# A hand-written planner orders the last stage of a three-stage kernel with a second set of machine constants and rules

## The chip, the cores and the metric

The kernel runs on one core of one Trainium2 chip. The metric is the device time of one execution in microseconds, here the median of three runs. Traces are of one profiled execution. The engines are called as the profile calls them: PE does matmuls (PEld is its weight loads), DVE, ACT and POOL do element-wise work, SP issues DMAs. Each engine runs its own list of instructions strictly in the order in which the program holds them, and semaphores make an instruction wait for work of other engines.

## What is computed

Three stages follow one another. The third is the one that the change is about.

```python
def _attn_ref(q, k, v):            # 4 x 8 heads, 576 positions, 64 wide, window of 128
    scores = where(mask, scale * q @ k.T + bias, -1e9)
    return softmax(scores) @ v
def _moe_ref(x, w_in, w_out):      # 2304 tokens, 512 -> 2048 -> 512
    h = np.maximum(x @ w_in, 0.0)
    return h * h @ w_out
def _moe2_ref(x, w_gate, w1, w2):  # 8 experts, 512 -> 1024 -> 512, all tokens through all
    P = sinkhorn(exp(x @ w_gate))  # 8 rounds
    out = 0
    for e in range(8):
        h = np.maximum(x @ w1[e], 0.0)
        out += P[:, e:e + 1] * (h @ w2[e])
    return out
```

## The kernel before

Nearly every fp32 matrix is held as two fp16 ones, a high and a low half, and a product is three fp16 matmuls (high-high, high-low, low-high). In the third stage each matrix product is done with seven block products in place of eight (sums and differences of blocks are formed first), so that PE does less and DVE, ACT and POOL do more.

**The third stage.** There are 16 groups `g` (8 experts in two halves), each with two parts `p`, and five blocks of tokens `j` (4, 2, 4, 4, 4 tiles of 128). For each `g, j, p`, `plan_pair` makes one pass: seven block products on PE (`g_prod`, L1450, six matmuls each) into the PSUM banks X, Y and Z; copies out of a bank by ACT (`g_copy`, L1478); additions of a bank to such a copy by DVE (`g_add`, L1482), on which the next product waits; relu and the high half by ACT (L1492, L1501, L1522); the low half by DVE (`g_lo`, L1526, from SBUF; `g_lo_bank`, L1505, straight from a bank); four running sums by POOL (`g_sum`, L407 and L1512). Seven output products follow for each block (`o_prod`, L1545, one after the other by a chain of dependences); DVE adds them into the result (`o_add`, L1571). Beside this the weights of the next group are prepared (`weights`): loaded (L1309), squared and summed for a scale (L1317), split in a high half by ACT (`ex_hi`, L1346) and a low half by DVE (`ex_lo`, L1350), with four block sums by POOL between the first and the second split (`ex_sums`, L1360 and L407). `gates` (L1682, L1683) makes the factors of a group on DVE.

**What sets the order.** Nothing is ordered by hand. Every piece of work is a `Unit` with an engine, a cost in us, a rank, the units it comes after, and the buffers it takes. `Plan.run` plays through a model of the machine: whenever an engine is free, it starts the ready unit of lowest rank. The order in which units start in this play is the order in which they are emitted, and so the order on each engine. Products have ranks that rise with `g`, `j` and `p`; the element-wise work of a pass has the first rank (`GEMM`); the preparation of weights comes last (9000 and up). Units `shared` (all of POOL's and those of DVE named in `PORT`: `g_lo`, `ex_lo` and others) exclude each other in the play: one that another engine's shared unit overlaps waits for its end. The result of a unit reaches its own engine after `own_lag` and another engine after `lags`. Buffers limit how far the play may run ahead: `h=2` banks (X, Y), `av=1` (Z), `y=4` (output banks), `hp=24` half pairs, `t=10` copies.

Costs are written as `c_pe(6, 256)` = 6 x (256/2400 + 0.0022) = 0.653 us for a product, `c_dve(n)` = 0.07 + 1.04 n/1000, `c_act(n)` = 0.18 + 0.83 n/1000 (0.18 replaced where a second number is given), `c_pool(n)` = 0.12 + 1.93 n/1000.

Of the kernel before, what the change touches and what calls it, by code (L numbers as in the profile page):

```python
# [18 lines left out]
class Unit:  # L19
    def __init__(self, engine, cost, emit, rank, lag, until):  # L20
        self.engine, self.cost, self.emit, self.rank, self.lag, self.until = engine, cost, emit, rank, lag, until
        self.name = ""
        self.waits, self.then, self.takes, self.nth, self.frees = 0, [], [], [], []
        self.shared = False


class Plan:
# [6 lines left out]
    def __init__(self, slots, queues):  # L34
        self.slots = slots
        self.queues = {tag: [] for tag in queues}
        self.units = []
        self.lags, self.own_lag = {}, {}
        self.got = {}

    def add(self, engine, cost, emit, after=(), rank=0, take=(), lag=None, until=None):
        u = Unit(engine, cost, emit, rank, self.lags.get(engine, 0.1) if lag is None else lag, until)
# [23 lines left out]
    def run(self):  # L66
        room = dict(self.slots)
        ready, free_at, events = {}, {}, []
        order, seq = [], 0

        def fits(u):
# [11 lines left out]
        held, until = None, 0.0  # L83
        while left:
            moved = True
            while moved:
                moved = False
                for eng, units in ready.items():
                    if free_at[eng] > now:
                        continue  # L90
                    fit = [
                        u for u in units if fits(u) and not (u.shared and held is not eng and until > now + 1e-6)
                    ]
# [4 lines left out]
                    if u.shared:  # L98
                        held, until = eng, now + u.cost
                    if u.until is not None and now > u.until:  # L100
                        u.cost, u.emit = 0.0, lambda: None
                    for t in u.takes:
# [3 lines left out]
                    free_at[eng] = now + u.cost  # L106
                    heapq.heappush(events, (now + u.cost, seq, eng, None))
                    heapq.heappush(events, (now + u.cost + self.own_lag.get(eng, u.lag), seq + 1, eng, (u, True)))
                    heapq.heappush(events, (now + u.cost + u.lag, seq + 2, eng, (u, False)))
                    seq += 3  # L110
# [7 lines left out]
            while events and events[0][0] <= now:  # L118
                u = heapq.heappop(events)[3]
                if u is None:  # L120
                    continue
                u, same = u
                for t in () if same else u.frees:
                    t[1] -= 1
                    room[t[0]] += not t[1]
                for x in u.then:
                    if same != (x.engine is u.engine):
                        continue
# [19 lines left out]
def kernel(  # L148
# [165 lines left out]
    def make_tail():  # L314
# [1033 lines left out]
    def ex_lo(g, kind, p, x):  # L1348
        for t, hi, lo in ex_parts(g, kind, p, x):
# [403 lines left out]
    def plan_pair(g, j, p, z, after, prev):  # L1753
# [3 lines left out]

        def split(name, *after):
# [6 lines left out]
                DVE, c_dve(n, 1.25 if of_bank else 1.04), g_lo_bank if of_bank else g_lo, g, j, p, name,  # L1765
                rank=GEMM, after=[hi],
            )
            fs[name] = (hi, lo)
            return lo

        def relu(x, after, **kw):
            return unit(ACT, c_act(n, 0.07), g_relu, g, j, p, x, rank=GEMM, after=[after], **kw)

        def total(name, *after):
            return unit(POOL, c_pool(n) + 0.08, g_sum, g, j, p, name, rank=GEMM, after=after)
# [3 lines left out]
        def prod(x, y, after, take=()):  # L1779
            return unit(PE, cost, g_prod, g, j, p, x, rank=z + 14 * y, take=take, after=after)  # L1780

        def copy(x, after):
            return unit(ACT, c_act(n, 0.06), g_copy, g, j, p, x, rank=GEMM, take=["t"], after=[after])

        def add(x, *after):
            return unit(DVE, c_dve(n), g_add, g, j, p, x, rank=GEMM, after=after)
# [41 lines left out]
    def plan_experts(closed, opened, lgt, routed):  # L1828
# [6 lines left out]
        def weights(g, kind):  # L1835
# [10 lines left out]
            us = chain(DVE, [0.14] + [TINY] * 3, ex_scale, g, kind, rank=z, after=[al])  # L1846
# [3 lines left out]
            for p in range(NP):  # L1850
# [8 lines left out]
                us.append(unit(DVE, c_dve(W, 1.17), ex_lo, g, kind, p, 1, rank=z + p, after=[hi]))  # L1859
# [82 lines left out]
    with tc.manual_schedule():  # L1942
# [33 lines left out]
        opened = unit(SP, 0.0, open_banks, after=[closed, *(u for us in ready_y.values() for u in us)])  # L1976
# [31 lines left out]
```

## Time and profile before

| | us |
|---|---|
| median of 3 runs (1927.27 to 1929.2) | 1928.04 |
| the profiled execution | 1927.08 |
| its span, first to last instruction | 1924.8 |
| PE busy in the span | 1887.3 |
| DVE busy in the span | 1540.3 |
| ACT, POOL busy in the span | 1239.8, 937.1 |

The profiled execution lies 0.96 us under the median and 2.28 us over its own span. Busy time of PE is the time in which at least one matmul is shown under way; a matmul's bar is longer than the distance to the next one, so that a run of matmuls is read by its starts. An idle time is put down to the work that released the instruction behind it.

### The profile page before, as it was taken

The numbers are of one execution on the slowest core, as the hardware profiler recorded it, in microseconds if no ns is written. First come the engines' busy times: TensorE is split into PE (matmuls) and PEld (weight loads), VectorE is DVE, ScalarE is ACT, GpSimd is POOL, SyncE is SP. The second block draws the span as 40 slices with busy tenths as digits, with TensorE's granted clock in tenths as the row PEclk, the third lists the DMA queues.
The fourth block names the chain that finished last, engine by engine and source line by source line (L and its number), as shares of the span: only waits on it lengthen the run. The fifth ranks groups of instructions, "written<-read, shape, count | busy, mean of one in ns | idle before, by whom it ended". The sixth has DMA issues, their size and how long they took to land.

```text
span 1924.8 us, 47113 instructions
## 1 busy us (share of the span) xinstructions
PE 1887.3 (98%) x18458; PEld 1681.8 (87%) x18458; DVE 1540.3 (80%) x3876; ACT 1239.8 (64%) x3434; POOL 937.1 (49%) x1198
## 2 busy tenths in 40 slices
PE   9999999999998999999999999999999999999998
PEld 9888888888887888898988889898888889888897
DVE  6796575454349889898988989899898889989877
ACT  5777577354356877676766667676666667666653
POOL 3444354347436655454545545454554545455432
PEclk9999999999999999999999999999999999999999
DMA  9454274220010100010100101010010101000002
GB/s 242 123 138 113 57 128 78 39 57 1 1 45 12 45 23 23 23 45 12 34 19 28 34 15 43 13 34 23 23 34 20 38 13 34 23 24 12 2 23 77
DMA packets 159662, 85.35 MB, mean 44 GB/s; under 512 B 112080, under 2 KB 144848, under 8 KB 159440
## 3 DMA queue, kind: packets, MB, share of 16 engines
q1 hardware_dynamic: 159440, 82.35, 17.0%
q8 instruction: 144, 2.36, 0.5%
q14 instruction: 78, 0.64, 0.1%
HBM read 64.50 MB, written 4.72 MB: 36 GB/s over the span
## 4 chain that ended last, share of the span: by engine, by line
PE 84%; DVE 10%; ACT 2%; DMA 2%; issue 1%; SPq 0%; POOL 0%; DVEq 0%; ACTq 0%; POOLq 0%
PE oX L1545 17%; PE X L1450 17%; PE oY L1545 9%; PE h L1036 9%; PE y L1075 8%; PE Y L1450 8%; PE Z L1450 5%; PE oZ L1545 4%; DVE hp L1526 3%; PE s L593 1%; PE warm L291 1%; DVE late L1350 1%; PE av L654 1%; DVE acc_wd L1571 1%; PE t L569 1%
## 5 line engine op out<-in xcount | busy, mean ns | idle before, releaser
L1450 PEld LDWEIGHTS <-late 128*128 128x128 f16 x6720 | 617.2, 98 | 89.5 <-issue 24.8
L1545 PEld LDWEIGHTS <-hp 128*128 128x128 f16 x6048 | 584.9, 98 | 64.9
L1545 PE MATMUL oX<-late,hp 128*128 128x256 f16 x3456 | 465.4, 273 | 0.0
L1450 PE MATMUL Y<-y,late 128*128 128x256 f16 (+1 forms) x1920 | 241.3, 262 | 5.1 <-DVE hp L1505 3.8
L1526 DVE TENSOR_TENSOR hp<-late,hp 128x256 f16<-128x256 f32 (+1 forms) x501 | 235.9, 485 | 5.6 <-ACT hp L1522 4.2
L1545 PE MATMUL oY<-late,hp 128*128 128x256 f16 x1728 | 235.2, 273 | 0.0
L1075 PE MATMUL y<-sq,w_out 128*128 128x256 f16 x1728 | 216.7, 273 | 1.4 <-DVE yacc L1089 0.9
L1036 PE MATMUL h<-xT,w_in 128*128 128x256 f16 x1728 | 215.9, 274 | 0.0
L1522 ACT ACTIVATE hp<-late 128x256 f16<-128x256 f32 (+1 forms) x501 | 193.8, 393 | 26.1 <-POOL late L407 13.8
L407 POOL TENSOR_TENSOR sq<-r,sq 128x256 f16<-128x256 f32 x144 | 105.1, 732 | 215.8 <-ACT sq L1061 214.5
L1450 PE MATMUL X<-late 128*128 128x256 f16 (+1 forms) x1728 | 204.9, 255 | 1.1 <-DVE late L1482 0.5
L407 POOL TENSOR_TENSOR stage<-stage 128x256 f32<-128x256 f32 x210 | 166.6, 799 | 75.4 <-DVE late L1350 64.2
L1036 PEld LDWEIGHTS <-w_in 128*128 128x128 f16 x1728 | 168.1, 98 | 20.8 <-issue 0.2
L1075 PEld LDWEIGHTS <-w_out 128*128 128x128 f16 x1728 | 166.2, 98 | 22.5 <-issue 2.4
L1450 PE MATMUL X<-form,late 128*128 128x256 f16 x1152 | 157.1, 272 | 13.6 <-DVE x L1482 6.9
L1350 DVE SCALAR_TENSOR_TENSOR late<-stage,es,late 128x512 f16<-128x512 f32 (+2 forms) x180 | 164.1, 937 | 0.6 <-ACT late L1346 0.5
L1492 ACT ACTIVATE late<-late 128x256 f32<-128x256 f32 (+1 forms) x206 | 79.7, 393 | 127.8 <-DVE late L1482 126.4
L1526 DVE TENSOR_TENSOR hp<-x,hp 128x256 f16<-128x256 f32 (+1 forms) x299 | 151.5, 516 | 3.2 <-ACT hp L1522 1.4
L1346 ACT ACTIVATE late<-stage,es 128x512 f16<-128x512 f32 (+2 forms) x180 | 135.6, 787 | 8.5 <-POOL stage L407 8.4
L407 POOL TENSOR_TENSOR late<-late 128x256 f32<-128x256 f32 (+1 forms) x167 | 126.6, 759 | 10.2
L1512 POOL TENSOR_TENSOR late<-late 128x256 f32<-128x256 f32 (+1 forms) x60 | 40.6, 677 | 182.4 <-DVE hp L1526 166.3
L1053 DVE SCALAR_TENSOR_TENSOR r<-h,unit_s,r 128x256 f32<-128x256 f32 x96 | 46.0, 480 | 101.6 <-ACT r L1045 101.1
(237 smaller groups left out, 3445.8 us busy)
## 6 DMA issues: line engine op xcount, KB each, us to landing
stage<-in_moe_w_dram SPq DMA_DIRECT2D x60, 256.0 KB, 3.2
stage<-in_moe_w_dram SPq DMA_DIRECT2D x30, 512.0 KB, 3.6
st_in<-in_moe_w_in_dram SPq DMA_DIRECT2D x16, 512.0 KB, 7.1
st_out<-in_moe_w_out_dram SPq DMA_DIRECT2D x16, 512.0 KB, 5.3
raw_q<-in_q_dram SPq DMA_DIRECT2D x16, 256.0 KB, 4.0
raw_k<-in_k_dram SPq DMA_DIRECT2D x16, 256.0 KB, 4.1
raw_v<-in_v_dram SPq DMA_DIRECT2D x16, 256.0 KB, 4.6
out_dram<-acc_wc SPq DMA_DIRECT2D x8, 256.0 KB, 2.3
```

Source lines behind the costliest of these rows:

```text
L407: POOL.tensor_tensor(out=dst, in0=src, in1=hi, op=ALU.subtract)
L1036: PE.matmul(hp, lhsT=w[:, a, kk, r], rhs=xT[parts1[m][0]][:, b, kk, c : c + MC], start=(kk == 0 and a == b), stop=(kk == KD - 1 and a == LO),)
L1053: DVE.scalar_tensor_tensor(out=r, in0=h if m > 1 else r, scalar=s, in1=r, op0=ALU.mult, op1=ALU.mult)
L1075: PE.matmul(hold["y", m, d // 2][:, d % 2], lhsT=w[:, a, f % FPC, d * P : (d + 1) * P], rhs=sq[:, b], start=(first and d % 2 == 0 and a == ...
L1346: ACT.activation(out=hi, in_=t, func=ACTF.Copy, scale=es[:, g, 2 * kind + 1 : 2 * kind + 2])
L1350: DVE.scalar_tensor_tensor(out=lo, in0=t, scalar=es[:, g, 2 * kind + 1 : 2 * kind + 2], in1=hi, op0=ALU.mult, op1=ALU.subtract)
L1450: PE.matmul(pt, lhsT=w[:, a, row(kk), :], rhs=rhs, start=(x in (1, 2, 5) and kk == 0 and a == c), stop=(x in (2, 3, 4) and kk == KH - 1 an ...
L1492: ACT.activation(out=t, in_=src, func=ACTF.Relu)
L1512: POOL.tensor_tensor(out=c, in0=c, in1=b, op=ALU.add)
L1522: ACT.activation(out=f[:, HI], in_=hold["t", PLACE[name], g, j, p], func=ACTF.Copy)
L1526: DVE.tensor_tensor(out=f[:, LO], in0=hold["t", PLACE[name], g, j, p], in1=f[:, HI], op=ALU.subtract)
L1545: PE.matmul(pt[:, t], lhsT=f[:, a, t * P : (t + 1) * P], rhs=w[:, c, row], start=(x in (1, 2, 5) and p == t == 0 and a == c), stop=(x in ( ...
```

## The change

The planner gets a second set of constants and three more rules; no instruction is added, dropped or altered, and only the order of instructions on the engines can differ.

- A `Model` holds the time that a result takes to another engine (`cross`) and to its own (`own`), a `lead` and a flag `turns`. The first model has the constants of before, lead 0 and no turns. `EXACT` has other constants, a lead of 0.065 us and turns. It takes over in the play when `open_banks` starts, that is when the last block of the second stage is split.
- `bank`: a unit that touches bank X, Y or Z of a pass can't start in the play while another engine's use of that bank, with its lag, is not over. This holds in both models.
- `lead`: a shared unit may start 0.065 us before the end of the one that it waits for. `turns`: an engine that has been refused the port goes before one that asks later.
- Costs: the low half from a bank 0.39 to 0.336 us (256 columns); relu 0.07 to 0.06 (bank) or 0.1 (SBUF) in its fixed part; `ex_lo`'s first split becomes two units of 512 and 256 columns in place of one (costed with 1024 or 768); `ex_scale` 0.14 + 3 x 0.08 to 4 x 0.07; sums on POOL 0.08 to 0.07 in the fixed part; `gates` 0.3 to 0.95.

```diff
+class Model:
+    def __init__(self, cross, own, lead, turns):
+        self.cross, self.own, self.lead, self.turns = cross, own, lead, turns
...
         def fits(u):
-            return all(
+            eng, until = banks.get(u.bank, (u.engine, 0.0))
+            if eng is not u.engine and until > now + 1e-6:
+                return False
+            if not all(
                 room[t[0]] > n and (t[0] not in self.queues or self.queues[t[0]][n] is u)
                 for t, n in zip(u.takes, u.nth)
+            ):
+                return False
+            if not u.shared:
+                return True
+            for eng, until in holds.items():
+                if eng is not u.engine and until > now + model.lead + 1e-6:
+                    wants.setdefault(u.engine, now)
+                    return False
+            since = wants.get(u.engine, now)
+            return not model.turns or all(
+                eng is u.engine or free_at[eng] > now or at >= since for eng, at in wants.items()
             )
...
-                    fit = [
-                        u for u in units if fits(u) and not (u.shared and held is not eng and until > now + 1e-6)
-                    ]
+                    fit = [u for u in units if fits(u)]
...
-                    if u.shared:
-                        held, until = eng, now + u.cost
+                    model = u.model or model
...
+                    there = end + (model.cross.get(eng, 0.1) if u.lag is None else u.lag)
+                    here = end + model.own.get(eng, 0.1 if u.lag is None else u.lag)
+                    push(here, [x for x in u.then if x.engine is eng])
+                    push(there, [x for x in u.then if x.engine is not eng])
+                    push(there, u)
+                    if u.bank is not None:
+                        banks[u.bank] = (eng, there)
...
+        Model({PE: 0.2, ACT: 0.22, DVE: 0.22, POOL: 0.22}, {PE: 0.0, ACT: 0.06, DVE: 0.06, POOL: 0.06}, 0.0, False),
     )
-    plan.lags.update({PE: 0.2, ACT: 0.22, DVE: 0.22, POOL: 0.22})
-    plan.own_lag.update({PE: 0.0, ACT: 0.06, DVE: 0.06, POOL: 0.06})
+    EXACT = Model(
+        {PE: 0.205, ACT: 0.16, DVE: 0.14, POOL: 0.1}, {PE: 0.0, ACT: 0.135, DVE: 0.115, POOL: 0.12}, 0.065, True
+    )
...
     def ex_lo(g, kind, p, x):
-        for t, hi, lo in ex_parts(g, kind, p, x):
+        for n, (t, hi, lo) in enumerate(ex_parts(g, kind, p, x)):
+            if n:
+                yield
...
-                DVE, c_dve(n, 1.25 if of_bank else 1.04), g_lo_bank if of_bank else g_lo, g, j, p, name,
+                DVE, c_dve(n), g_lo_bank if of_bank else g_lo, g, j, p, name,
                 rank=GEMM, after=[hi],
             )
+            if of_bank:
+                at(OF_BANK[name], hi)
+                at(OF_BANK[name], lo)
...
         def prod(x, y, after, take=()):
-            return unit(PE, cost, g_prod, g, j, p, x, rank=z + 14 * y, take=take, after=after)
+            return at(PROD[x][0], unit(PE, cost, g_prod, g, j, p, x, rank=z + 14 * y, take=take, after=after))
...
-            return unit(DVE, c_dve(n), g_add, g, j, p, x, rank=GEMM, after=after)
+            return at({"a": "Z", "b": "Y", "c": "X"}[x], unit(DVE, c_dve(n), g_add, g, j, p, x, rank=GEMM, after=after))
...
-            us = chain(DVE, [0.14] + [TINY] * 3, ex_scale, g, kind, rank=z, after=[al])
+            us = chain(DVE, [0.07] * 4, ex_scale, g, kind, rank=z, after=[al])
...
-                us = [unit(DVE, c_dve(n1, 1.17), ex_lo, g, kind, p, 0, rank=z + p, after=[hi])]
-                u = chain(POOL, [c_pool(2 * P) + 0.08] * 4, ex_sums, g, kind, p, rank=z + p, after=us)[-1]
+                us = chain(DVE, [c_dve(2 * HD, 1.17), c_dve(HD, 1.3)], ex_lo, g, kind, p, 0, rank=z + p, after=[hi])
+                u = chain(POOL, [c_pool(2 * P) + 0.07] * 4, ex_sums, g, kind, p, rank=z + p, after=us[-1:])[-1]
...
-                gated[g] = unit(DVE, 0.3, gates, g, rank=8000, after=[routed, scales[g, 0], scales[g, 1]])
+                gated[g] = unit(DVE, 0.95, gates, g, rank=8000, after=[routed, scales[g, 0], scales[g, 1]])
...
-        opened = unit(SP, 0.0, open_banks, after=[closed, *(u for us in ready_y.values() for u in us)])
+        opened = switch = unit(SP, 0.0, open_banks, after=[closed, *(u for us in ready_y.values() for u in us)])
+        switch.model = EXACT
```

## Rows read from the trace of the kernel before

**Rows 1.** Stretches: length, busy us (instructions) of PE, PEld, DVE, ACT, POOL; clock; DMA.

```profile
0.00:396.50 396.50, 387.80 (x4013) 336.01 (x4014) 266.84 (x796) 259.61 (x690) 170.96 (x194) 1.00 0.52 113
396.50:580.00 183.50, 177.92 (x1753) 158.72 (x1752) 81.49 (x196) 88.64 (x216) 102.21 (x127) 1.00 0.08 24
580.00:700.00 120.00, 115.61 (x1097) 102.13 (x1095) 108.06 (x259) 91.57 (x250) 75.33 (x90) 0.99 0.11 32
1149.00:1233.00 84.00, 83.11 (x802) 74.88 (x802) 75.82 (x187) 56.29 (x160) 41.98 (x56) 1.00 0.09 26
1822.00:1920.00 98.00, 97.22 (x930) 87.37 (x929) 78.04 (x195) 50.70 (x150) 31.50 (x44) 1.00 0.11 39
```

**Rows 2.** Waits of PE from 700 us to the end: total us, times, longest.

```profile
PE X L1450 <- DVE x L1482: 6.3, 7, 0.9
PE X L1450 <- DVE late L1482: 5.9, 8, 0.9
PE Y L1450 <- DVE hp L1505: 1.7, 2, 0.9
```

**Rows 3.** Waits of PE from 580 to 700 us, the two largest.

```profile
PE Y L1450 <- DVE hp L1505: 1.7, 3, 1.1
PE X L1450 <- DVE late L1482: 1.3, 1, 1.3
```

**Rows 4.** Timeline of PE about one wait: start, us, instruction, idle before.

```profile
1230.75 0.82 PE L1545 MATMUL oX<-late,hp 128*128 128x256 f16 x6
1231.40 0.82 PE L1545 MATMUL oY<-late,hp 128*128 128x256 f16 x6
1233.11 0.81 PE L1450 MATMUL X<-form,late 128*128 128x256 f16 x6 [0.89 <-DVE x L1482]
1233.76 0.82 PE L1545 MATMUL oY<-late,hp 128*128 128x256 f16 x6
1234.42 0.82 PE L1450 MATMUL X<-y,late 128*128 128x256 f16 x6
```

**Rows 5.** Timeline of DVE and POOL ahead of the same wait.

```profile
1228.38 0.83 DVE L1526 TENSOR_TENSOR hp<-late,hp 128x256 f16<-128x256 f32 x1
1229.01 2.52 POOL L407 TENSOR_TENSOR stage<-stage 128x256 f32<-128x256 f32 x3
1230.01 0.94 DVE L1526 TENSOR_TENSOR hp<-late,hp 128x256 f16<-128x256 f32 x1
1232.32 0.41 DVE L1526 TENSOR_TENSOR hp<-late,hp 128x256 f16<-128x256 f32 x1
1232.65 0.41 DVE L1482 TENSOR_TENSOR x<-X,x 128x256 f32<-128x256 f32 x1
```

**Rows 6.** Timeline of one bank's readers, and of POOL's sums, for the distances between engines.

```profile
1223.54 0.82 PE L1450 MATMUL X<-form,late 128*128 128x256 f16 x6
1224.40 0.38 ACT L1501 ACTIVATE hp<-X 128x256 f16<-128x256 f32 x1 [0.64 <-PE X L1450]
1224.68 0.38 ACT L1492 ACTIVATE late<-X 128x256 f32<-128x256 f32 x1
1225.09 0.43 DVE L1505 SCALAR_TENSOR_TENSOR hp<-X,hp 128x256 f16<-128x256 f32 x1 [0.79 <-ACT late L1492]
...
1906.94 0.73 POOL L407 TENSOR_TENSOR x<-x,late 128x256 f32<-128x256 f32 x1
1907.71 0.42 ACT L1522 ACTIVATE hp<-x 128x256 f16<-128x256 f32 x1 [0.39 <-POOL x L407]
```

**Rows 7.** Groups of DVE, 750 to 1800 us: count, busy us, mean ns, idle before.

```profile
L1526 DVE TENSOR_TENSOR hp<-late,hp 128x256 f16<-128x256 f32 x314 | 161.8, 527 | 1.1
L1526 DVE TENSOR_TENSOR hp<-x,hp 128x256 f16<-128x256 f32 x183 | 100.7, 559 | 2.7 <-ACT hp L1522 1.0
```

**Rows 8.** The factors of a group on DVE: count, min/median/max ns, first and last start.

```profile
L1683 DVE SCALAR_TENSOR_TENSOR pd<-prob,gs,typ x14: 243/788/795, 671.0 to 1750.6; 128x18 f32<-128x18 f32 x14
```

**Rows 9.** Waits of PE from 396.5 to 580 us, the three largest.

```profile
PE total L265 <- DVE es L243: 1.5, 1, 1.5
PE total L265 <- DVE prob L1620: 1.4, 1, 1.4
PE Y L1450 <- ACT late L1478: 1.2, 1, 1.2
```

**Rows 10.** Timeline of the last instructions.

```profile
1919.92 0.87 DVE L1571 SCALAR_TENSOR_TENSOR x<-oX,pd,x 128x256 f32<-128x256 f32 x2 [0.43 <-PE oX L1545]
1920.43 1.54 SPq L1584 DMA_DIRECT2D out_dram<-x  x3
```

More of the change, by code (lines that the diff above doesn't have):

```diff
@@ L23, in __init__ @@
         self.waits, self.then, self.takes, self.nth, self.frees = 0, [], [], [], []
-        self.shared = False
+        self.shared, self.bank, self.slow, self.model = False, None, False, None
+class Model:
+    def __init__(self, cross, own, lead, turns):
+        self.cross, self.own, self.lead, self.turns = cross, own, lead, turns
 class Plan:
-    def __init__(self, slots, queues):
+    def __init__(self, slots, queues, model):
         self.slots = slots
@@ L37, in __init__ @@
         self.units = []
-        self.lags, self.own_lag = {}, {}
+        self.model = model
         self.got = {}
     def add(self, engine, cost, emit, after=(), rank=0, take=(), lag=None, until=None):
-        u = Unit(engine, cost, emit, rank, self.lags.get(engine, 0.1) if lag is None else lag, until)
+        u = Unit(engine, cost, emit, rank, lag, until)
         self.units.append(u)
@@ L69, in run, with push @@
         order, seq = [], 0
+        holds, wants, banks = {}, {}, {}
+        model = self.model
         def fits(u):
-            return all(
+            eng, until = banks.get(u.bank, (u.engine, 0.0))
+            if eng is not u.engine and until > now + 1e-6:
+                return False
+            if not all(
                 room[t[0]] > n and (t[0] not in self.queues or self.queues[t[0]][n] is u)
                 for t, n in zip(u.takes, u.nth)
-            )
+            ):
[9 more added lines that the diff above has]
+                eng is u.engine or free_at[eng] > now or at >= since for eng, at in wants.items()
+            )
+        def push(at, what):
+            nonlocal seq
+            heapq.heappush(events, (at, seq, what))
+            seq += 1
         for u in self.units:
@@ L97, in run @@
                     units.remove(u)
-                    if u.shared:
-                        held, until = eng, now + u.cost
+                    model = u.model or model
                     if u.until is not None and now > u.until:
                         u.cost, u.emit = 0.0, lambda: None
+                    end = free_at[eng] = now + u.cost
+                    push(end, None)
+                    wants.pop(eng, None)
+                    if u.shared:
+                        holds[eng] = end
+                        push(max(now, end - model.lead), None)
                     for t in u.takes:
@@ L118, in run @@
             while events and events[0][0] <= now:
-                u = heapq.heappop(events)[3]
-                if u is None:
-                    continue
[L122 to L128, printed above, removed]
+                what = heapq.heappop(events)[2]
+                if isinstance(what, Unit):
+                    for t in what.frees:
+                        t[1] -= 1
+                        room[t[0]] += not t[1]
+                    continue
+                for x in what or ():
                     x.waits -= 1
@@ L1756, in plan_pair, with at @@
         fs = {}
+        def at(b, u):
+            u.bank = (b, g, j, p)
+            return u
         def split(name, *after):
@@ L1771, in relu @@
         def relu(x, after, **kw):
[L1772 removed]
+            b = {"a": "Z", "X": "X"}.get(x)
+            u = unit(ACT, c_act(n, 0.06 if b else 0.1), g_relu, g, j, p, x, rank=GEMM, after=[after], **kw)
+            return at(b, u) if b else u
         def total(name, *after):
[L1775 removed]
+            return unit(POOL, c_pool(n) + 0.07, g_sum, g, j, p, name, rank=GEMM, after=after)
         cost = c_pe(6, n)
         def prod(x, y, after, take=()):
[L1780 removed]
+            return at(PROD[x][0], unit(PE, cost, g_prod, g, j, p, x, rank=z + 14 * y, take=take, after=after))
         def copy(x, after):
[L1783 removed]
+            u = unit(ACT, c_act(n, 0.06), g_copy, g, j, p, x, rank=GEMM, take=["t"], after=[after])
+            return at("Y" if x == "c" else "X", u)
         def add(x, *after):
[L1786 removed]
+            return at({"a": "Z", "b": "Y", "c": "X"}[x], unit(DVE, c_dve(n), g_add, g, j, p, x, rank=GEMM, after=after))
         p1 = prod(1, 0, [*after, *prev], ["h"])
```

8 lines of the change are left out of this document (1 added, 7 removed).

## The prediction

> **What bounds the kernel now.** I read the stretches first. PE is busy for 387.8 of the first 396.5 us, 177.9 of the next 183.5, 115.6 of 120 us while the third stage starts, then 83.11 of 84 us in one of its groups, and 97.2 of the last 98 us [rows 1]. The next engine, DVE, has 75.8 us of the 84. So PE bounds the kernel nearly everywhere, DVE comes close behind it in the third stage, and an order can win only what PE still waits.
>
> How much that is I read from the waits of PE. From 700 us to the end there are 6.3 + 5.9 + 1.7 = 13.9 us in 17 waits, all on DVE: 15 on an addition (L1482), 2 on a low half taken from a bank (L1505) [rows 2]. From 580 to 700 us the same kinds make most of some 4 us [rows 3], with three waits under 0.7 us beside them. Thirteen of the 17 are one wait repeated, once in each 84 us from 813 to 1823 us, each shown as 0.9 us.
>
> One of them in detail. The six matmuls of a block product start 0.65 us after the six before them when nothing holds them (1230.75 to 1231.40); the held one starts at 1233.11, 1.71 us after 1231.40, so the wait costs 1.71 - 0.65 = 1.06 us, 0.16 more than the 0.89 shown [rows 4], because a matmul's bar runs on past the next one's start. By this measure the 17 waits cost 13.9 + 17 x 0.16 = 16.6 us. The two lines behind decide what can be had. The next instruction on PE, oY at 1233.76, is the second half (p = 1) of the output product begun at 1231.40. Its input is the first of POOL's running sums, and the oX at 1230.75 needed the third of the same chain for the same p, which is formed from it. So by these dependences oY could have run at 1232.05, when PE fell idle [rows 4]. PE had work; its list had it in the wrong place.
>
> Why the play put it there: ahead of the wait DVE is late. Three low halves take 0.83 to 0.94 us while three sums of POOL run beside them, against 0.41 us for the same instruction a little later; the addition that PE waits for comes at 1232.65, with no idle time of DVE before it [rows 5], where two of the three slow ones stand. The old play also holds these two kinds apart, but with other costs and lags.
>
> **The change, part by part.** No instruction is removed or added. The same matmuls remain, so PE's own work of some 83 us a group stays; only waits can go or come.
>
> Constants. I compare with distances between starts. PE to ACT: the product starts at 1223.54, ACT reads its bank at 1224.40, 0.86 us; the new set says 0.653 + 0.205 = 0.858, the old 0.853. ACT to DVE: 1224.68 to 1225.09, 0.41; new 0.2725 + 0.16 = 0.43, old 0.2825 + 0.22 = 0.50. POOL to ACT: 1906.94 to 1907.71, 0.77; new 0.684 + 0.10 = 0.78, old 0.694 + 0.22 = 0.91 [rows 6]. DVE to PE: 1232.65 to 1233.11, 0.46; new 0.336 + 0.14 = 0.476, old 0.556 [rows 4, 5]. The new play is right within 0.02 us at all four places, and where it errs it is on the safe side; the old one is 0.08 to 0.14 us too slow at three. A play that is right about when an addition lands takes oY ahead of the held product.
>
> Bank. At 1225.09 DVE's low half waits for ACT's second read of the same bank (L1492), not for the high half that it needs [rows 6]: the program's semaphores already keep two engines off one bank. The rule teaches the play a wait that exists, and adds none.
>
> Turns and lead. Low halves and POOL's sums alternate at 0.8 to 0.9 us a pair [rows 5]; the new rule plays that.
>
> Smaller costs. The factors of a group take 0.79 us in their second instruction alone [rows 8] where the old play has 0.3 for both; 0.95 is nearer. The split in two of the first low half of weights lets an addition go between, worth at most the second piece's 0.4 us where the two meet.
>
> Now the sum. Thirteen regular waits of 1.06 us: a ready oY covers 0.65 of each, and the next output product may cover the rest, but then it is a coin's toss whether the held one starts late by a fraction; I take 0.85 each, 11.0 us (bounds 0.65 and 1.06: 8.5 to 13.8). The other four of the 17, some 2.2 us with 0.16 each (16.6 less 13.8 is 2.8): I take 0.9. The start from 580 to 700 us: DVE is busy 108 of 120 us and cannot be emptied by order alone, so a quarter of some 5.3 us (4.2 shown, 7 waits of 0.16 more), 1.3 us (bounds minus 2, since a new order may add as much, and 4). From 396.5 to 580 us the old constants still hold, but weights of the first group are prepared there with new costs; PE waits 4 us in three places [rows 9], the first behind work whose cost in the play changes by 0.1 us, the others behind none that changes: I take 0, bounds plus and minus 2. Ahead of that nothing changes in the play: both sets of rules are the same there. At the end PE's last product is followed by one addition and one output [rows 10], untouched. Sum: 11.0 + 0.9 + 1.3 = 13.2 us. The profiled execution would take 1927.08 - 13.2 = 1913.9, the median, 0.96 above it, 1914.8 us.
>
> **A rule that speaks against it.** The wait that returns every 84 us is on PE's list, with another output product directly behind it whose input was there [rows 4]. The Trainium skill (Perfetto Trace Analysis, Optimization Strategy) reads it otherwise: consistent bubbles, the same gap repeating on the engine that should be saturated, can mean that there isn't enough SBUF or PSUM for the next tile. By that rule the change, which leaves all buffers as they are, would win nothing of the regular part and the time would stay near 1927. The trace agrees with the regularity, but what ends the wait is an addition on DVE, not the release of a buffer; so it stands among the rivals.
>
> **The rivals.** (1) The waits only move. The play is still limited by two banks, ten copies and 24 halves, and what PE takes early at one place it lacks at the next; or the regular wait is a buffer's after all (the rule above). For it: the wait's exact return. Against it: 17 waits on DVE, none on a buffer's release, save the two on L1505 [rows 2]. Price: of the 13.2 us saved 10 to 15 are lost again, so 1925 to 1930, about 1927.
>
> (2) Slower: DVE becomes the bound through the port. In 1050 us there are 314 + 183 = 497 low halves of full width, 40 in each 84 us, of (161.8 + 100.7) / 497 = 0.528 us on average [rows 7], against 0.41 alone and 0.94 beside POOL [rows 5]; so some (0.528 - 0.41) / 0.53 = 22%, 9 of 40, meet POOL now. DVE has 83 - 75.8 = 7.2 us to spare in a group. If the new order, with its shorter lags, brings 14 more of the 40 beside a sum, 14 x 0.53 = 7.4 us, the room is gone; each one beyond costs 0.53 x 14 groups = 7.4 us. Two beyond give +15, about 1943; and since DVE can't use all of its idle time, the loss starts earlier, from some 1933. For it: shorter lags take away 0.08 to 0.14 us of slack at each of hundreds of dependences. Against it: the rule of turns lets DVE choose work that reads a bank while POOL holds the port.
>
> (3) More than forecast: the exact play also dissolves the start and all of each regular wait: 16.6 + 4 + 2 = 22.6 us, about 1905.
>
> (4) The change doesn't do what it says: the second model takes over at the opening of the banks, some 580 us, so all the regular waits lie behind the switch; I see no way in which it stays without effect, and count it with (1).
>
> **How the numbers follow.** The forecast's own range, by its bounds, goes from 1928.04 - (13.8 + 4 + 2) = 1908 to 1928.04 - (8.5 - 2 - 2) = 1924: 0.64. Rival (1): 0.17. Rival (2): 0.15. Rival (3): 0.04. A measurement of this kernel tells 0.2%, 3.9 us, from no change: faster than 1924.2 has 0.64 + 0.04 = 0.68, within it 0.17, slower than 1931.9 0.15. The range reaches from 1904, just below rival (3), to 1932, the end of rival (1); it leaves out rival (2), 0.15, and little below.
>
> **What would show it.** Right: PE's waits from 700 us on fall from 13.9 us to under 4; the distance between the starts of one group and the next falls from 84.0 to 83.2 us or less; PE's order has the second oY ahead of the held product; DVE's busy time in a group stays within 2 us of 75.8. Wrong in the step of the ready oY: the regular wait is still there, at another product. Wrong in the step of the constants: many waits of 0.05 to 0.3 us in place of one of 0.9. Wrong by the port: the mean of L1526 rises beyond 0.6 us and waits on L1526 appear on PE. Wrong about the start: the stretch from 580 to 700 us has less PE work than now.

## The result, and the profile after

The changed kernel takes 1911.83 us (median of 6 runs, 1910.16 to 1914.24) where the one before took 1928.55 beside it (6 runs); the ratio is 0.9916, with a 95% interval of 0.9903 to 0.9929. The profiled execution took 1910.95 us, its span is 1909.1 us, 15.7 less than before. 1914.8 us were forecast.

In the changed kernel most lines stand 31 further down: the block product L1450 is L1481, the addition L1482 is L1513, low halves L1526 and L1505 are L1557 and L1536, the output product L1545 is L1576, the low half of weights L1350 is L1381, and the helper of POOL's sums, L407, is L436.

Where the time went is read from one instruction that returns in every group: the first block product of the second block of tokens, which is half as wide (128x128). First the kernel before, then after (timeline: start, us, instruction), at the first, second and last of its 16 places.

```profile
570.61 0.50 PE L1450 MATMUL X<-y,late 128*128 128x128 f16 x6
...
663.10 0.50 PE L1450 MATMUL X<-y,late 128*128 128x128 f16 x6
...
1842.31 0.50 PE L1450 MATMUL X<-y,late 128*128 128x128 f16 x6
```

```profile
569.62 0.50 PE L1481 MATMUL X<-y,late 128*128 128x128 f16 x6
...
659.68 0.49 PE L1481 MATMUL X<-y,late 128*128 128x128 f16 x6
...
1826.61 0.50 PE L1481 MATMUL X<-y,late 128*128 128x128 f16 x6
```

Up to the first place 1.0 us is won; between the first two (the start) 92.49 - 90.06 = 2.4; over the next 14 groups (the steady part) 1179.21 - 1166.93 = 12.3; from the last place to the end (82.49 us in both) nothing. Together 15.7 us, the whole difference of the spans. Six groups in a row now take 82.91 us each, where [rows 4] belong to groups of 84.0.

Two stretches after, with the columns of [rows 1]: one whole group, and the start of the third stage.

```profile
1160.40:1243.30 82.90, 82.90 (x805) 74.83 (x802) 72.56 (x186) 56.74 (x161) 41.61 (x56) 1.00 0.09 27
...
580.00:700.00 120.00, 115.09 (x1091) 101.70 (x1089) 107.59 (x253) 92.35 (x253) 72.75 (x91) 1.00 0.09 28
```

PE is without idle time in that group. DVE, with the same instructions, is busy for 72.6 us in it, against 75.8 [rows 1]. In the start DVE is as busy as before, PE does a little less from 580 to 700 us (115.1 us against 115.6), and its waits there add up to 4.6 us where they were 4.2. Most of the 2.4 us won in the start is the clock of PE. Five us of both kernels, before and after, with the same columns:

```profile
580.00:585.00 5.00, 5.00 (x50) 3.96 (x48) 4.90 (x16) 1.96 (x8) 3.50 (x5) 0.67 0.01 3
...
580.00:585.00 5.00, 5.00 (x56) 4.44 (x54) 5.00 (x11) 2.63 (x11) 3.68 (x5) 1.00 0.01 3
```

Before, the granted clock stood at 0.50 (1.2 GHz) from about 580 to 583 us, behind a stretch in which PE was busy for 6.08 of 9.39 us (570.61 to 580); after, it stays at 1.00 (2.4 GHz), behind 8.14 busy us of 10.38. By the mean of 0.67 the low clock cost some 5 x 0.33 = 1.65 us, an estimate. That the new order kept the clock up is not tested by itself; of the runs that start in the old order, e1 and e10 show the same fall (0.66) and e9 doesn't.

The waits of PE from 700 us on (total, times, longest) answer to [rows 2]:

```profile
PE X L1481 <- ACT x L1509: 1.4, 1, 1.4
PE total L292 <- ACT bands L1346: 0.8, 1, 0.8
PE X L1481 <- DVE x L1513: 0.6, 1, 0.6
PE Y L1481 <- ACT x L1509: 0.3, 1, 0.3
```

Of 13.9 us in 17 waits, 3.1 us in 4 are left, and the one that returned every 84 us is gone. So far the prediction holds. Its reason for the regular wait doesn't. This is the same place of the same group after the change, to be laid beside [rows 4, 5] (timeline of PE, DVE and POOL):

```profile
1217.95 0.75 DVE L1381 SCALAR_TENSOR_TENSOR late<-stage,es,late 128x512 f16<-128x512 f32 x1
1218.24 1.06 POOL L436 TENSOR_TENSOR x<-x,late 128x256 f32<-128x256 f32 x1
...
1218.97 0.95 DVE L1557 TENSOR_TENSOR hp<-x,hp 128x256 f16<-128x256 f32 x2
...
1221.96 0.47 DVE L1381 SCALAR_TENSOR_TENSOR late<-stage,es,late 128x256 f16<-128x256 f32 x1
...
1222.40 0.42 DVE L1513 TENSOR_TENSOR late<-X,late 128x256 f32<-128x256 f32 x1
1222.56 0.73 POOL L1391 TENSOR_TENSOR stage<-stage 128x256 f32<-128x256 f32 x1 [3.26 <-ACT late L1523]
...
1222.86 0.82 PE L1576 MATMUL oY<-late,hp 128*128 128x256 f16 x6
...
1223.51 0.82 PE L1481 MATMUL X<-form,late 128*128 128x256 f16 x6
...
1224.16 0.82 PE L1576 MATMUL oY<-late,hp 128*128 128x256 f16 x6
...
1224.82 0.82 PE L1481 MATMUL X<-y,late 128*128 128x256 f16 x6
```

PE's order is what it was: oY, the block product, oY, the next pass. The block product simply no longer waits. What moved is on DVE. The two pieces of the low half of weights, one unit before, now lie 4.0 us apart (1217.95 and 1221.96), with additions and low halves between them. POOL's four block sums need the second piece, so they begin at 1222.56, behind most of the low halves, where before they began among them [rows 5].

### The profile page after: what moved, and what is told of

Same layout as the page of the kernel before. It is cut to its first block, busy times and chain, and to the rows that moved or that the text cites. A ratio compares the mean times of both kernels' runs of the same rounds, so it can differ in the third digit from the quotient of the medians.

```text
span 1909.1 us, 47140 instructions
## 1 busy us (share of the span) xinstructions
PE 1883.0 (99%) x18458; PEld 1680.5 (88%) x18458; DVE 1495.1 (78%) x3876; ACT 1248.7 (65%) x3434; POOL 928.5 (49%) x1198
## 4 chain that ended last, share of the span: by engine, by line
PE 62%; DVE 1%; DMA 1%; ACT 1%; issue 0%; POOL 0%; SPq 0%; DVEq 0%; ACTq 0%
PE oX L1576 18%; PE X L1481 18%; PE oY L1576 9%; PE Y L1481 9%; PE oZ L1576 4%; PE Z L1481 4%; DMA stage<-in_moe_w_dram 1%; DVE hp L1557 0%; ACT bands L1346 0%; DVE late L1381 0%; PE total L292 0%; ACT hp L1553 0%; ACT acc_wc L1610 0%; DVE acc_wc L1602 0%; DVE x L1513 0%
## 5 line engine op out<-in xcount | busy, mean ns | idle before, releaser
L1481 PEld LDWEIGHTS <-late 128*128 128x128 f16 x6720 | 617.8, 98 | 75.1 <-issue 9.9
L1576 PEld LDWEIGHTS <-hp 128*128 128x128 f16 x6048 | 583.6, 98 | 64.6 <-issue 0.8
L1576 PE MATMUL oX<-late,hp 128*128 128x256 f16 x3456 | 466.1, 273 | 0.5 <-ACT acc_wd L1597 0.3
L1481 PE MATMUL Y<-y,late 128*128 128x256 f16 (+1 forms) x1920 | 241.4, 262 | 2.8 <-ACT late L1509 1.4
L1576 PE MATMUL oY<-late,hp 128*128 128x256 f16 x1728 | 235.2, 273 | 0.0
L1557 DVE TENSOR_TENSOR hp<-late,hp 128x256 f16<-128x256 f32 (+1 forms) x482 | 212.1, 451 | 14.1 <-ACT hp L1553 12.1
L1481 PE MATMUL X<-late 128*128 128x256 f16 (+1 forms) x1728 | 204.7, 255 | 3.3 <-DVE x L1513 1.7
L436 POOL TENSOR_TENSOR sq<-r,sq 128x256 f16<-128x256 f32 x144 | 104.4, 727 | 212.3 <-ACT sq L1090 203.1
L1553 ACT ACTIVATE hp<-late 128x256 f16<-128x256 f32 (+1 forms) x482 | 185.5, 394 | 31.6 <-POOL late L1543 14.5
L436 POOL TENSOR_TENSOR stage<-stage 128x256 f32<-128x256 f32 x210 | 163.2, 778 | 9.1 <-ACT x L1523 1.4
L1481 PE MATMUL X<-form,late 128*128 128x256 f16 x1152 | 157.1, 273 | 0.8 <-DVE late L1513 0.7
L1381 DVE SCALAR_TENSOR_TENSOR late<-stage,es,late 128x512 f16<-128x512 f32 (+2 forms) x180 | 155.2, 864 | 1.3 <-ACT late L1375 1.3
L1557 DVE TENSOR_TENSOR hp<-x,hp 128x256 f16<-128x256 f32 (+1 forms) x318 | 142.5, 455 | 6.7 <-ACT hp L1553 5.7
L1523 ACT ACTIVATE late<-late 128x256 f32<-128x256 f32 (+1 forms) x195 | 75.1, 389 | 103.9 <-DVE late L1513 101.8
L1553 ACT ACTIVATE hp<-x 128x256 f16<-128x256 f32 (+1 forms) x318 | 123.8, 396 | 20.7 <-POOL x L1543 9.9
L436 POOL TENSOR_TENSOR late<-late 128x256 f32<-128x256 f32 (+1 forms) x174 | 126.5, 728 | 10.0
```

Source lines behind the costliest of these rows:

```text
L436: POOL.tensor_tensor(out=dst, in0=src, in1=hi, op=ALU.subtract)
L1381: DVE.scalar_tensor_tensor(out=lo, in0=t, scalar=es[:, g, 2 * kind + 1 : 2 * kind + 2], in1=hi, op0=ALU.mult, op1=ALU.subtract)
L1481: PE.matmul(pt, lhsT=w[:, a, row(kk), :], rhs=rhs, start=(x in (1, 2, 5) and kk == 0 and a == c), stop=(x in (2, 3, 4) and kk == KH - 1 an ...
L1523: ACT.activation(out=t, in_=src, func=ACTF.Relu)
L1553: ACT.activation(out=f[:, HI], in_=hold["t", PLACE[name], g, j, p], func=ACTF.Copy)
L1557: DVE.tensor_tensor(out=f[:, LO], in0=hold["t", PLACE[name], g, j, p], in1=f[:, HI], op=ALU.subtract)
```

## The experiments

All ratios are to the kernel before on the same chip, with 95% intervals; "us" is the difference that the ratio makes of 1928. "Steady us" is the difference from the kernel before in the time from the second of the 16 places to the last, read from one trace of each run: it leaves out the start, where the clock of PE fell in some runs and not in others. What each run was meant to do follows the table.

| run | what it is | ratio | us | steady us |
|---|---|---|---|---|
| changed kernel | | 0.9916 [0.9903, 0.9929] | -16.2 | -12.3 |
| e1_swap | before, 13 pairs exchanged on PE | 0.9995 [0.9986, 1.0003] | -1.0 | +0.1 |
| e2_only_lags | before + new lags | 1.0064 [1.0050, 1.0077] | +12.3 | +14.5 |
| e3_only_bank | before + bank rule | 1.0016 [1.0007, 1.0024] | +3.1 | +0.3 |
| e4_only_turns | before + turns and lead | 0.9966 [0.9954, 0.9978] | -6.6 | -6.5 |
| e5_no_turns | changed - turns and lead | 0.9937 [0.9925, 0.9950] | -12.1 | -5.1 |
| e6_no_lags | changed - new lags | 0.9952 [0.9940, 0.9965] | -9.3 | -8.4 |
| e7_no_bank | changed - bank rule | 0.9945 [0.9932, 0.9959] | -10.6 | -10.2 |
| e8_no_costs | changed - costs and split | 0.9959 [0.9946, 0.9973] | -7.9 | -7.0 |
| e9_narrow_sums | before, POOL's block sums narrow | 0.9912 [0.9896, 0.9927] | -17.0 | -15.8 |
| e10_narrow_adds | before, some of DVE's additions narrow | 0.9958 [0.9941, 0.9974] | -8.1 | -7.5 |
| e11_twice | changed, more work for DVE | 0.9967 [0.9953, 0.9981] | -6.4 | -4.6 |
| e12_plus_port | changed, more users of the port | 0.9892 [0.9874, 0.9910] | -20.8 | -17.7 |

### Was it PE's list?

The prediction's step was tried by itself: the kernel before with nothing altered but the two neighbours on PE.

```diff
+        at = {u.name: n for n, u in enumerate(order) if u.name}
+        for g in range(2, 15):
+            a, b = at["g_prod", (g, 4, 1, 4)], at["o_prod", (g, 3, 1, 5)]
+            order[a : b + 1] = [*order[a + 1 : b + 1], order[a]]
```

> The kernel before with 13 pairs of neighbours exchanged on PE alone, one in each group from g = 2 to 14: the output product o_prod(g, 3, p=1, 5) now stands ahead of the block product g_prod(g, 4, p=1, 4) that waited 1.06 us. Nothing else is moved, all buffers and all other engines' orders are those of before. Theory (PE's list was wrong, the work was there): the regular wait falls from 1.06 us to 0.0 to 0.4 us, PE's waits after 700 us from 13.9 to under 5, the time by 8 to 13 us to 1915 to 1920. Rival (a buffer is missing, as its regular return suggests): the wait comes back at the next product, the time stays within 2 us of before.

Nothing is won, though the exchange did what it was to do. Timeline of PE in this run at the old wait, and 22 us later:

```profile
1232.64 1.47 PE L1550 MATMUL oY<-late,hp 128*128 128x256 f16 x12
1234.37 0.82 PE L1455 MATMUL X<-form,late 128*128 128x256 f16 x6 [0.25 <-DVE x L1487]
...
1256.19 0.49 PE L1455 MATMUL Y<-y,late 128*128 128x128 f16 x6 [0.55 <-DVE hp L1510]
```

Both oY now run in one, so the input was there, as forecast, and the old wait falls from 0.89 to 0.25 us. But another appears, on a bank that DVE has not yet read out. PE's waits from 700 us on:

```profile
PE Y L1455 <- DVE hp L1510: 7.7, 12, 0.8
PE X L1455 <- DVE late L1487: 2.2, 9, 0.3
PE X L1455 <- DVE x L1487: 1.7, 7, 0.3
PE total L270 <- ACT bands L1322: 0.3, 1, 0.3
```

They add up to 11.9 us in 29 pieces in place of 13.9 in 17, and most groups still take 84.0 to 84.3 us. This reads as if DVE were late by about 1 us in each group and PE paid it somewhere, its own list saying only where; e9 tests it. The rival had the time right; that a buffer was missing remained possible until e9.

### Which part of the change?

Each part alone, added to the kernel before, and each alone taken from the changed one. As edits of the changed kernel they are short, here, in this order, e5, e6, e7 and the part of e8 that joins the split low half again (e8 has all the old costs besides):

```diff
-        {PE: 0.205, ACT: 0.16, DVE: 0.14, POOL: 0.1}, {PE: 0.0, ACT: 0.135, DVE: 0.115, POOL: 0.12}, 0.065, True
+        {PE: 0.205, ACT: 0.16, DVE: 0.14, POOL: 0.1}, {PE: 0.0, ACT: 0.135, DVE: 0.115, POOL: 0.12}, 0.0, False
...
-        {PE: 0.205, ACT: 0.16, DVE: 0.14, POOL: 0.1}, {PE: 0.0, ACT: 0.135, DVE: 0.115, POOL: 0.12}, 0.065, True
+        {PE: 0.2, ACT: 0.22, DVE: 0.22, POOL: 0.22}, {PE: 0.0, ACT: 0.06, DVE: 0.06, POOL: 0.06}, 0.065, True
...
-            u.bank = (b, g, j, p)
...
-            if n:
-                yield
```

> The kernel before with the new lags alone from the switch on (cross and own of EXACT, lead 0, no turns), without the bank rule and with all old costs. Theory (the right landing times put PE's list right): most of the gain, 8 to 14 us less than before, the regular wait gone. Rival (the misjudged port and costs on DVE made the list wrong, the lags didn't): under 4 us, the regular wait still there at some product.

> The kernel before with the rule of one engine a bank alone; lags, costs, lead and turns are the old ones. Theory (the lags carry the gain): under 4 us either way, a regular wait remains. Rival (the play missed waits between the readers of a bank, and these made DVE late): 8 to 14 us less.

> The kernel before with the rule of turns and the lead of 0.065 us alone; lags, costs and banks are the old ones. Theory (the lags carry the gain): under 4 us either way. Rival (low halves that meet POOL's sums made DVE late): 8 to 14 us less, with low halves (L1526 before) at a mean under 0.50 us in place of 0.53 to 0.56.

The lags, on which the prediction built most, make the kernel slower by 12 us when they come alone. Waits of PE from 700 us on in e2:

```profile
PE X L1479 <- DVE late L1511: 8.2, 15, 0.6
PE X L1479 <- DVE x L1511: 5.9, 11, 0.6
```

There are now two waits in most groups where there was one, and a group takes 85.2 to 85.4 us; neither expectation of e2 allowed for a loss. The bank rule alone costs 3 us, nearly all of it ahead of the steady part (0.3 there). Turns and lead alone win 6.6, between what the theory (under 4) and the rival (8 to 14) expected: the one part that is about the port helps by itself. Low halves in e4 and in the changed kernel, 750 to 1750 us, columns as in [rows 7]:

```profile
L1555 DVE TENSOR_TENSOR hp<-late,hp 128x256 f16<-128x256 f32 x292 | 138.7, 490 | 6.7 <-ACT hp L1551 6.6
L1555 DVE TENSOR_TENSOR hp<-x,hp 128x256 f16<-128x256 f32 x184 | 88.7, 490 | 3.8 <-ACT hp L1551 3.7
```

```profile
L1557 DVE TENSOR_TENSOR hp<-late,hp 128x256 f16<-128x256 f32 x285 | 134.7, 485 | 3.5 <-ACT hp L1553 1.5
L1557 DVE TENSOR_TENSOR hp<-x,hp 128x256 f16<-128x256 f32 x197 | 95.0, 489 | 2.5 <-ACT hp L1553 1.5
```

A low half takes 0.49 us on the mean in both, where it took 0.53 to 0.56 [rows 7]: fewer of them meet a sum of POOL's.

> The changed kernel without the rule of turns and without the lead; all else as changed. Theory after the first four runs (what went is DVE's time at the port, and only a play that knows the port spaces low halves and POOL's sums): 5 to 14 us are lost again, 1917 to 1926, low halves back at a mean over 0.52 us. Rival (the pieces add up, turns alone gave 5.6): 1917.5. Rival (the rest of the set suffices): within 3 us of 1912.

> The changed kernel with the old lags from the switch on; bank rule, lead, turns and costs as changed. Theory (the lags matter only where the port is played right; alone they cost 12 us): 3 to 8 us are lost, 1915 to 1920. Rival (the pieces add up): 12 us better than the changed kernel, about 1900. Rival (they don't matter beside the rest): within 3 us of 1912.

> The changed kernel without the rule of one engine a bank. Theory (with short lags the play now starts DVE's reading of a bank while ACT still reads it, a wait that the program really has): 3 to 10 us are lost, 1915 to 1922, with PE's waits on low halves from a bank (L1505 before) up. Rival (the pieces add up, the rule alone cost 3): about 1909.

> The changed kernel with all costs of before and the first low half of weights in one unit. Theory (costs are a small correction beside the port and the lags): 2 to 6 us are lost, 1914 to 1918. Rival (the pieces add up: lags +12, bank +3, turns -6 leave -26 for the costs): about 1938.

Taken from the whole, the lags cost 6.9 us, the bank rule 5.6, costs and split 8.3, turns and lead 4.0 (for these last the intervals of e5 and of the changed kernel overlap by 0.0004). So e6 and e7 came out as their theories had it, e8 lost a little more than 2 to 6, and e5 a little less than 5 to 14, near the sum of the pieces. The parts don't add up; by adding, e8 would have been at 1938, and it is 8 us faster than before.

In the steady part, where the regular wait was, the parts rank otherwise. Taken from the whole, turns and lead cost 12.3 - 5.1 = 7.2 us there, costs and split 5.3, the lags 3.9, the bank rule 2.1; alone, turns and lead win 6.5, the bank rule does next to nothing, and the lags lose 14.5. There the rule about the port is the largest part both ways. The second and the last place in e5:

```profile
658.01 0.50 PE L1481 MATMUL X<-y,late 128*128 128x128 f16 x6
...
1832.17 0.50 PE L1481 MATMUL X<-y,late 128*128 128x128 f16 x6
```

That is 1174.16 us, against 1166.93 with turns and lead. Low halves in e5 and in e8 (750 to 1750 us):

```profile
L1557 DVE TENSOR_TENSOR hp<-late,hp 128x256 f16<-128x256 f32 x280 | 147.7, 536 | 5.1 <-ACT hp L1553 3.6
L1557 DVE TENSOR_TENSOR hp<-x,hp 128x256 f16<-128x256 f32 x196 | 106.6, 547 | 3.8 <-ACT hp L1553 3.0
...
L1555 DVE TENSOR_TENSOR hp<-late,hp 128x256 f16<-128x256 f32 x282 | 134.8, 492 | 4.4 <-ACT hp L1551 4.4
L1555 DVE TENSOR_TENSOR hp<-x,hp 128x256 f16<-128x256 f32 x197 | 92.3, 474 | 3.5 <-ACT hp L1551 3.5
```

In e5 they take as long as before, and 5.1 us of the steady part are won all the same; in e8 they are as short as in the changed kernel, and it loses 5.3 us of the steady part. So the time lost at the port in all is not the whole measure; it also matters whether it falls where DVE has something due. And e8 has no split: its block sums follow the low half of weights at once again, but at the like place only one low half from SBUF stands beside them, where there were three [rows 5], and additions that read a bank stand there at their usual 0.86 us for two (timeline of DVE and POOL):

```profile
1222.95 0.73 POOL L1389 TENSOR_TENSOR stage<-stage 128x256 f32<-128x256 f32 x1 [0.36 <-DVE late L1379]
1223.13 0.83 DVE L1555 TENSOR_TENSOR hp<-x,hp 128x256 f16<-128x256 f32 x1
1223.76 2.41 POOL L436 TENSOR_TENSOR stage<-stage 128x256 f32<-128x256 f32 x3
1223.88 0.86 DVE L1600 SCALAR_TENSOR_TENSOR acc_wd<-oZ,pd,acc_wd 128x256 f32<-128x256 f32 x2
```

So the split is one way in which low halves and block sums come apart, and not the only one.

### What makes DVE late?

The old order was then kept whole, on every engine, and one cost taken out of it at a time.

```diff
-            a11, a12, a21, a22 = t[:, :KH, 0], t[:, KH:, 0], t[:, :KH, 1], t[:, KH:, 1]
+            a11, a12, a21, a22 = t[:, :KH, 0, :8], t[:, KH:, 0, :8], t[:, :KH, 1, :8], t[:, KH:, 1, :8]
...
-            b11, b12, b21, b22 = t[:, 0, :HD], t[:, 0, HD:], t[:, 1, :HD], t[:, 1, HD:]
+            b11, b12, b21, b22 = t[:, 0, :16], t[:, 0, HD : HD + 16], t[:, 1, :16], t[:, 1, HD : HD + 16]
```

> The kernel before, every list in its old order; of the four block sums that POOL makes for each prepared weight only 16 of 256 columns are computed (the rest of the sums is left out). DVE's own work is the same, POOL holds the port less. Theory (DVE is behind by about 1 us in one stretch of each group, because its low halves meet these sums at the port, and PE pays that wherever its list stands): the regular wait of 1.06 us goes without any reordering, 8 to 14 us less, 1914 to 1920, low halves (L1526) under 0.48 us on the mean. Rival (the sums at the port don't matter, the lists of PE and the banks do): within 3 us of before.

With the old lists, the old buffers and the old work of DVE, 17 us go, more than the 8 to 14 expected. Timeline of DVE and POOL in this run at the place of [rows 5] (lines as before):

```profile
1222.35 0.41 DVE L1526 TENSOR_TENSOR hp<-late,hp 128x256 f16<-128x256 f32 x1
1222.47 1.07 POOL L407 TENSOR_TENSOR stage<-stage 128x16 f32<-128x16 f32 x3
1222.68 0.43 DVE L1526 TENSOR_TENSOR hp<-x,hp 128x256 f16<-128x256 f32 x1
1223.04 0.43 DVE L1526 TENSOR_TENSOR hp<-late,hp 128x256 f16<-128x256 f32 x1
```

The three low halves that took 0.83 to 0.94 us take 0.41 to 0.43; PE's waits from 700 us on are 1.2 us in three pieces, and most groups take 82.9 us, as in the changed order with the full sums. Over 750 to 1750 us the mean of the low halves falls from 0.54 to 0.49 us, just short of the 0.48 expected. Narrow sums also give POOL time back, but POOL was not what was late there. In the kernel before it stands idle behind the block sums until DVE has a low half ready:

```profile
1234.49 0.73 POOL L1512 TENSOR_TENSOR x<-x,late 128x256 f32<-128x256 f32 x1 [2.96 <-DVE hp L1526]
```

So the regular wait was DVE's delay at the port, among low halves and block sums. The Trainium skill (SBUF, Who interferes with whom) says that a DVE instruction with two SBUF inputs contends with a GpSimd instruction that reads SBUF. The trace agrees: a low half takes 0.41 us alone and 0.94 beside a sum. The cause that the Trainium skill (Perfetto Trace Analysis, Optimization Strategy) names for consistent bubbles, missing buffers, is not the one here: the wait went in e9 and in the change, and no buffer was added in either.

```diff
+            w = 16 if x in (2, 6) else HD
             for t in range(n):
                 DVE.scalar_tensor_tensor(
-                    out=A[:, t], in0=pt[:, t], scalar=pd[:, g, i + t : i + t + 1], in1=A[:, t], op0=ALU.mult, op1=ALU.add
+                    out=A[:, t, :w], in0=pt[:, t, :w], scalar=pd[:, g, i + t : i + t + 1], in1=A[:, t, :w], op0=ALU.mult, op1=ALU.add
```

> The kernel before, every list in its old order; of the additions of output products (g from 2 on) those of two of seven products work on 16 of 256 columns (the rest is left out). This takes about 1 us of DVE's own work from each block of tokens, 5 us a group, and leaves the port as it was. Theory (DVE is behind in one stretch of each group, whatever its work there is): the regular wait goes, 8 to 14 us less, 1914 to 1920. Rival (only collisions at the port make the wait): within 3 us of before.

8 us go, the low end of what the theory expected, but the regular wait only halves: PE's waits on additions are 5.6 us in 14 pieces in place of 12.2 in 15, a group takes 83.5 us. DVE's own work in that stretch is part of the delay too. A group wins 0.5 us for 3.7 us less of DVE's busy time (72.1 us; 5 us less were aimed at), so most of the work taken out lies where nothing waits. The rival's zero misses.

### How much room is there now?

```diff
-            DVE.scalar_tensor_tensor(
+            for _ in range(2 if (kind, p, x) == (0, 0, 1) else 1):
+                DVE.scalar_tensor_tensor(
```

> The changed kernel, every list in its new order; in each group DVE makes one low half of weights (1024 columns, kind 0, p = 0) twice, 1.27 us more for DVE. Theory (in the new order DVE has more than this to spare where the weights are prepared): under 5 us slower, 1912 to 1917. Rival (the new order stands as close to the edge as the old one and every microsecond of DVE is paid by PE): 15 x 1.27 = 19 us slower, about 1931.

About 10 us slower than the changed kernel, between the two: 1.27 us more for DVE in a group cost some 0.6. Groups take 83.4 us in place of 82.9; the list of PE's waits from 700 us on shows 2.9 us in 5 pieces, so it doesn't tell where this goes. The new order is not safe from more work, though DVE is idle for 10 us in a group.

```diff
-    PORT = {"g_lo", "ex_lo", "t_lo", "v_lo", "x_lo", "x_hi", "narrow", "join_v", "prep_gate", "h_square"}
+    PORT = {"g_lo", "ex_lo", "t_lo", "v_lo", "x_lo", "x_hi", "narrow", "join_v", "prep_gate", "h_square", "sink_rows", "sink_columns", "gates"}
-                gated[g] = unit(DVE, 0.95, gates, g, rank=8000, after=[routed, scales[g, 0], scales[g, 1]])
+                gated[g] = unit(DVE, 0.4, gates, g, rank=8000, after=[routed, scales[g, 0], scales[g, 1]])
```

> The changed kernel with three more kinds of DVE's work declared as users of the port in the play (the rows and columns of the sinkhorn rounds, and the factors of a group, these at 0.4 us in place of 0.95). Theory (a play that also knows these collisions orders the start better): of some 7 us of waits from 580 to 750 us up to 3 go, 1909 to 1912. Rival (the rest of the waits is not of this kind, and another order is as good or bad as another): 1912 plus or minus 5.

1908.32 us, the fastest of all here. Its waits of PE from 580 to 700 us, where the changed kernel has 4.6 us:

```profile
PE lg L1632 <- DVE y L1172: 1.0, 2, 0.6
PE Y L1481 <- ACT late L1509: 0.2, 1, 0.2
```

So the start is better ordered by a play that knows these collisions, as the theory had it: 3.4 us of waits go, and from the first of the 16 places to the third it takes 169.5 us where the changed kernel takes 175.0. From there to the last place the two are alike (1081.9 and 1082.0 us). The profiled execution doesn't show the gain in its whole length, 1910.61 us, since it comes to the first place 5.35 us later than the changed kernel's; its granted clock was 0.98 in the first 396.5 us, against 1.00. Whether the whole beats the changed kernel is not settled: the intervals of the two ratios overlap (0.9874 to 0.9910, and 0.9903 to 0.9929).

## Why the prediction was right, and where it wasn't

**The size.** By the places of the section on the result: from the second place to the last 12.3 us, where the steady waits were put at 11.0 + 0.9; the start 2.4, where 1.3 was taken; ahead of it 1.0, where 0 plus or minus 2 was taken; the end 0. The bounds of each term hold, and the sum of 13.2 was 2.5 too small, mostly in the start and ahead of it. The other four waits of the 17 stand there as 2.2 and as 2.8 us in one sentence (2.2 is what the list shows, 2.8 has 0.16 us for each); the 0.9 taken lies within both. The agreement is in part luck. The 0.85 us for each regular wait was worked out from a ready oY that was not what covered it, and the start's term counted on fewer waits, where the waits are no shorter than before and some 1.65 (an estimate) of the 2.4 us are the clock, which no term has.

**What bounds the kernel.** Right in the steady part: PE's waits were what there was to win, and 12.3 of 16.6 us went. Of the signs named, two came (waits under 4 us, a group of 83.2 us or less), and three spoke against the account: the order of PE, DVE's busy time, and a little less PE work from 580 to 700 us than before.

**The ready oY.** This step failed: "PE had work; its list had it in the wrong place". The first half is true (e1 ran it there), the second is not: e1 won nothing, and the changed kernel has the old order on PE at this place. The sign named for it, the second oY ahead of the held product, did not come. The step priced the wait as if PE could spend it elsewhere; but DVE was behind, and when PE went on, the next thing that DVE was late for was a bank (7.7 us in 12 waits on L1510 in e1). What covered the wait is DVE: low halves that meet POOL's block sums take up to 0.94 us in place of 0.41, and with the sums narrow the wait goes in the old order (e9).

**The constants.** They were read rightly off the trace, but the conclusion that a play with right landing times orders better was false by itself: e2 is 12 us slower. That shorter lags take slack away stood among the arguments of rival (2), and it may be what decided there; no run tests it. In company the same constants win (3.9 us in the steady part, e6).

**The bank rule, turns and costs.** "Adds none": the rule teaches an existing wait, yet alone it costs 3 us and in company wins 5.6, in the steady part 2.1 (e3, e7). Turns and lead got no price of their own, and in the steady part they are the largest of the four (e4, e5). The split in two was priced at up to 0.4 us "where the two meet"; with the costs it is worth 8.3 us, 5.3 of them in the steady part (e8). The runs don't tell the split from the other costs.

**The rivals.** (2) named the right place, low halves beside sums at the port, with the other sign: the new order brings fewer together, and DVE's busy time in a group falls by 3.2 us. That was more than the 2 us within which the prediction wanted it to stay, and a sign that the gain came by DVE. (1) came true for e1, where the waits only moved. (3)'s dissolved start is seen in part in e12.

## What to carry to other kernels

A wait on the busiest engine that returns with each round can be a delay of the engine that it waits for, as here: before the busiest engine's list is mended, move one instruction; if the time stays, look for what makes the other engine late. Here low halves and block sums cost time when they met, and what helped was an order of the two engines that kept them apart, in e8 with additions that read a bank beside the sums instead. Constants and rules of a planner are to be timed as a set as well as one by one: the new lags are a loss alone and a gain in company, so trying them by themselves would have dropped them. And a difference of a few us in the whole should be divided by stages before it is put down to a part: by the whole, turns and lead look like the smallest of the four, in the steady part they are the largest.

## What the hardware showed that was not expected

The cost of a collision is not that of large instructions alone. The factors of a group, 128x18, took 0.79 us at the median [rows 8]. Timeline of the kernel before at one of them:

```profile
741.34 0.79 DVE L1683 SCALAR_TENSOR_TENSOR pd<-prob,gs,typ 128x18 f32<-128x18 f32 x1
741.37 0.73 POOL L407 TENSOR_TENSOR late<-late 128x256 f32<-128x256 f32 x1
```

A sum of POOL's begins 0.03 us after it and ends 0.03 us before it. In the changed kernel, 750 to 1750 us, no sum meets it, and it takes a third:

```profile
L1714 DVE SCALAR_TENSOR_TENSOR pd<-prob,gs,typ 128x18 f32<-128x18 f32 x12 | 2.9, 244 | 0.4
```

So the 0.95 us of the change's play has the wait in the price; e12 gives it 0.4 us and the port instead. And a DVE instruction's bar holds the time that it loses at the port (0.24 us and 0.79 for the same instruction), so that DVE's busy time, 75.8 us in a group of before, was 3.2 us less for the same instructions in another order.
